# Attention and two gated layers on one core: the integer adds and subtractions of the weight conversions on VectorE, and VectorE's order after the attention as written

## The chip, the core and the metric

The kernel runs on one core of a Trainium2 chip. The core has TensorE (PE, matmuls; PEld is its loading of weights), VectorE (DVE), ScalarE (ACT), GpSimd (POOL) and SyncE (SP), which here issues all DMAs. Each engine takes its own instructions in a fixed order; semaphores hold an instruction until what it needs is there. The metric is the device time of the program in microseconds (us). All times below are us unless marked ns.

## The reference

Four batches of eight heads go through an attention with a window of 128 positions, and the result through two gated layers:

```python
x = attention(q, k, v)             # (4, 8, 576, 64) -> 2304 tokens x 512; window 128, slopes by head
x = ((x @ w_a) * (x @ w_b)) @ w_out            # 512 -> 1536 -> 512
h = ((x @ w1) * (x @ w2)) @ w3                 # 512 -> 1024 -> 1024
out = h @ moe2_w_out                           # 1024 -> 512
```

The weights come as 64-bit floats, read by the kernel as pairs of 32-bit words.

## The kernel before

Every fp32 operand of a matmul is split into a high half, rounded to the matmul's format (fp32r), and a low half, the difference. A product is three matmuls: high x low, low x high, high x high. Layer 1 has six groups of weights (0 to 5) and layer 2 four (6 to 9). A group holds two chunks of 128 columns, each with three parts: of `w_a` (z = 0), of `w_b` (z = 1) and of the output matrix (z = 2), as tiles `whA0`, `wlA0`, `whA1`, `wlA1` for even groups and with B for odd ones. w3 and moe2_w_out are multiplied on the chip to one matrix in two halves (`w34_parts`), and each product goes through DRAM (`w34`); layer 2 adds the halves again (L507).

**A weight's conversion** (`convert`, `split`) makes 128 x 512 fp32 of a `raw` tile of 64-bit words:
- a DMA into `raw`, of which there are two (L82, L91);
- stage s0 on ACT: L107 takes the upper word to `ca` (three buffers), L110 makes a rounding addend `ce` of the lower word (one buffer);
- stage s1 on DVE: L114, L117 and L121 build the fp32 pattern; after L121 and L110 the `raw` is free and its next DMA may start;
- stage s3: L126 adds `ce` to `ca` as integers; then `ce` is free;
- the last stage, `split`: L133 on ACT makes the high half, L72 (in the helper `sub`) the low half. For w3 there are instead four transposes on PE (L437), a high half on ACT (L438), a low half on DVE (L439), and twelve matmuls (L445), whose result ACT copies into a `ce` buffer (L447) for the store to DRAM.

`Stages.turn` advances all conversions that are under way by one stage and starts at most one new; at most three are under way. In the groups a tile of 512 tokens calls it through `side.run` about 3.8 times. Before, L126 and the L72 of conversions ran on POOL, except for group 0's, which ran on DVE (`eng`).

**A group's work on a tile** of 512 tokens: `g1`, four times twelve matmuls (L532) into four PSUM banks; ACT copies a product (L539), DVE multiplies by the other (L541, tile `g`), ACT makes the high half (L544, `gh`) and POOL the low half (L72, `gl`). Then the second product, four banks of six matmuls (L560 in group 0, L571 in groups 1 to 5, L586 after), which DVE adds to `acc` (L575, L593; L591 copies). It runs one tile later, behind the next tile's `g1`. In group 5, ACT and POOL make `x_hi` and `x_lo` of the sum (L577, L72). Group 0 has tiles of 256 tokens; its work fills gaps in the attention, and the rest comes right after it (L740), followed in the text by all of group 1's conversions (L743 to L745) and then by groups 1 to 9 (L751). After the attention there are eight PSUM banks for the matmuls, two in one pool and six in another, taken in turn.

**What sets the order.** A scheduler orders each engine's instructions by dependencies and its own estimates of time. A `manual_schedule` block keeps chosen engines in the order of the text: before, that was PE during the attention alone (L715 to L731). After it all engines, DVE too, were ordered by the scheduler.

Of the kernel before, what the change touches and what calls it, by code (L numbers as in the profile page):

```python
# [16 lines left out]
ALU = mybir.AluOpType  # L17
# [9 lines left out]
def bits(x):  # L27
    return struct.unpack("<f", struct.pack("<I", x))[0]
# [15 lines left out]
def attention_moe_moe(ctx, tc, q, k, v, w_a, w_b, w_o, w_1, w_2, w_3, w_o2, out):  # L44
    nc = tc.nc
# [10 lines left out]
    W = 512  # L56
# [11 lines left out]
    def f32(ap):  # L68
        return ap.bitcast(F32)

    def sub(eng, out, a, b):
        eng.tensor_tensor(out=out, in0=a, in1=b, op=ALU.subtract)  # L72
# [6 lines left out]
    def load_cols(w, c):  # L79

        raw = pools["conv"].tile([P, W, 2], I32, name="raw", bufs=pools["raws"])
        nc.sync.dma_start(  # L82
            out=raw.rearrange("p (k f) t -> p k (f t)", k=KC),
            in_=w[:, c * P:(c + 1) * P].bitcast(I32).rearrange("(k p) f -> p k f", p=P),
        )
        return raw

    def load_rows(w, r, c):

        raw = pools["conv"].tile([P, W, 2], I32, name="raw", bufs=pools["raws"])  # L90
        nc.sync.dma_start(  # L91
            out=raw.rearrange("p f t -> p (f t)"),
            in_=w[r * P:(r + 1) * P, c * W:(c + 1) * W].bitcast(I32),
        )
        return raw

    def convert(raw, hi=None, lo=None, use=(), eng=None):


        hw, lw = raw[:, :, 1], raw[:, :, 0].bitcast(U32)  # L100
        a = pools["conv"].tile([P, W], F32, name="ca", bufs=pools["cas"])
        ai = a.bitcast(I32)
        es = []

        def s0():

            nc.scalar.activation(a, f32(hw), ACTF.Abs)  # L107
            e = pools["conv"].tile([P, W], I32, name="ce", bufs=1)
            es.append(e)
            nc.scalar.activation(e, lw, ACTF.Copy, scale=2.0 ** -29)  # L110

        def s1():

            nc.vector.tensor_scalar(  # L114
                out=a, in0=a, scalar1=bits(0x38000000), scalar2=None, op0=ALU.max
            )
            nc.vector.tensor_scalar(  # L117
                out=ai, in0=ai, scalar1=3, scalar2=0x3FFFFFF8,
                op0=ALU.logical_shift_left, op1=ALU.bitwise_and,
            )  # L120
            nc.vector.scalar_tensor_tensor(  # L121
                out=ai, in0=hw, scalar=-(1 << 30), in1=ai, op0=ALU.bitwise_and, op1=ALU.bitwise_or
            )

        def s3():
            (eng or nc.gpsimd).tensor_tensor(out=ai, in0=ai, in1=es[0], op=ALU.add)  # L126

        if hi is None:
            return [s0, s1, s3] + [lambda f=f: f(a) for f in use]
        return [s0, s1, s3, lambda: split(a, hi, lo, eng)]  # L130

    def split(f, hi, lo, eng=None):
        nc.scalar.activation(hi, f, ACTF.Copy)  # L133
        sub(eng or nc.gpsimd, lo, f, f32(hi))

    class Stages:

# [125 lines left out]
    def prep(run, n):  # L263
        b, (x, i) = blocks_of(run)[0], items(run)[n]
        m = rows(i)
        hold = []

        def trans():
            ps = ps_t.tile([P, W], F32, name="tr")[:, 0:NP * m].rearrange("p (h c) -> p h c", h=NP)
            hold.append(ps)  # L270
            t = raws.pop((b, x, i))
            for hp in range(NP):
                nc.tensor.transpose(ps[:, hp, :], t[0:m, hp * P:(hp + 1) * P], ident[0:m, 0:m])  # L273

        def parted():
            ps = hold[0]
            if x == 0 and m == LAST:
                dst = [(slice(j * D, (j + 1) * D), q_t2, slice(j * D, (j + 1) * D)) for j in range(2)]
            else:
                dst = [(slice(0, P), k_t if x else q_t, slice(i * P, i * P + m))]  # L280
            for o, (hi, lo), c in dst:
                nc.scalar.activation(hi[o, :, c], ps[o], ACTF.Copy)
                sub(nc.vector, lo[o, :, c], ps[o], f32(hi[o, :, c]))

        return trans, parted
# [137 lines left out]
    def w34_parts(pool, halves):  # L423
# [28 lines left out]
        for half in halves:  # L452
            for j in range(NJ):
                parts.append((
                    lambda r=half * NJ + j: load_rows(w_o2, r, 0),
                    lambda raw, j=j: convert(raw, oh[:, j, :], ol[:, j, :]),
                ))
            for f in range(FB):
                parts.append((
                    lambda f=f, half=half: load_rows(w_3, f, half),  # L460
                    lambda raw, f=f, half=half: convert(raw, use=product(half, f)),
                ))
# [10 lines left out]
    def weight_parts(g):  # L473

        blk, chunks = groups[g]
        d = blocks[blk]
        ring = "AB"[g % 2]

        def load(n, z):
            c = chunks[n]  # L480
            if z == 0:
                wt[g, n] = [
                    pools[ring, n].tile([P, 3, KC, P], F32R, name=f"w{s}{ring}{n}", bufs=1) for s in "hl"
                ]
            if z < 2:
                return load_cols(d["ab"[z]], c)
            if blk == 0:
                return load_rows(d["o"], c, 0)
            raw = pools["conv"].tile([P, W, 2], I32, name="raw", bufs=pools["raws"])
            raw = raw.rearrange("p f t -> p (f t)").bitcast(F32)  # L490
            for half in range(2):
                nc.sync.dma_start(
                    out=raw[:, half * W:(half + 1) * W], in_=d["o"][half, c * P:(c + 1) * P, :]
                )
            return raw

        def stages(raw, n, z):
            hi, lo = [t[:, z].rearrange("p k f -> p (k f)") for t in wt[g, n]]

            def count():  # L500
                whole[g] = whole.get(g, 0) + 1

            if z < 2 or blk == 0:
                return convert(raw, hi, lo, eng=None if g else nc.vector) + [count]

            def add():
                nc.gpsimd.tensor_tensor(out=raw[:, 0:W], in0=raw[:, 0:W], in1=raw[:, W:2 * W], op=ALU.add)  # L507

            return [add, lambda: split(raw[:, 0:W], hi, lo), count]

        return [
            (lambda n=n, z=z: load(n, z), lambda raw, n=n, z=z: stages(raw, n, z))
            for n in range(2) for z in range(3)
        ]
# [189 lines left out]
    for x in range(len(items(1))):  # L704
        load_item(1, x)
        f, g = prep(0, x)
# [30 lines left out]
    pools["B", 0] = pools["B", 1] = ctx.enter_context(tc.tile_pool(name="wB", bufs=1))  # L737
    ps_h = ctx.enter_context(tc.tile_pool(name="ps_h", bufs=6, space=PSUM))
    pools["mm"] = [ps_g, ps_h, ps_h, ps_h]
    for f, _, _ in fl.items:  # L740
        side.turn()
        f()
# [35 lines left out]
```

## Time and profile before

| | |
|---|---|
| median of three runs | 977.05 us (974.28 to 977.43) |
| profiled execution | 978.53 us, of which the span is 976.8 |
| PE | busy 944.9 us (97%), 5546 matmuls |
| DVE | 516.5 us (53%) |
| ACT | 417.2 us (43%) |
| POOL | 341.7 us (35%) |
| DMA | 68.30 MB, 24% of 16 engines |
| attention | until about 229 us |
| chain that ended last | PE 84%, DVE 7%, DMA 6%, ACT 2% |

A timeline row has the start, the length, the engine, the line, the operation, output and inputs, and how many in a row; in brackets stands how long the engine was idle before it, and which instruction ended that. "PEclk" is the clock that TensorE was granted, 1.00 for 2.4 GHz and 0.50 for 1.2 GHz. Lengths of matmuls overlap, so that their rate is read from starts.

### The profile page before, as it was taken

The page shows a single profiled execution, that of the slowest core. Times are in us where ns is not written, and L with a number is a line of the kernel's source. Part 1 is how long each engine was busy: PE and PEld are TensorE (multiplying, and loading weights), DVE is VectorE, ACT ScalarE, POOL GpSimd, SP SyncE. Part 2 cuts the span into 40 slices and gives each one's busy share as a digit, 9 for nine tenths or more (in the row PEclk, how much of TensorE's full clock was granted, in tenths as well). Part 3 has the DMA queues.
Part 4 walks back from the last instruction along what each step waited for, and adds up shares of the span by engine and source line. Part 5 has one row for each costly group of instructions (what it writes and reads, how often), then busy time and mean ns, then how long its engine had stood idle before and what let it go on. Part 6 is the DMA issues. An engine that isn't in the chain of part 4 may idle for free.

```text
span 976.8 us, 14512 instructions
## 1 busy us (share of the span) xinstructions
PE 944.9 (97%) x5546; PEld 797.1 (82%) x5546; DVE 516.5 (53%) x1177; ACT 417.2 (43%) x951; POOL 341.7 (35%) x285
## 2 busy tenths in 40 slices
PE   7699999999989999999999999999999999999998
PEld 5487888889777888888888888888888888888886
DVE  6968686865887435756564462542541541421322
ACT  6767787775654323543533441342421321311111
POOL 3000000003776223744542462683831631511111
PEclk8899999999999999999999999999999999999999
DMA  9623231102343122413322330210210210000012
GB/s 212 171 55 74 60 86 40 33 2 94 123 124 114 45 86 76 135 71 98 125 70 84 97 110 1 87 44 1 67 64 1 87 44 0 22 1 1 33 65 97
DMA packets 90373, 68.30 MB, mean 70 GB/s; under 512 B 58304, under 2 KB 79296, under 8 KB 90304
## 3 DMA queue, kind: packets, MB, share of 16 engines
q1 hardware_dynamic: 90304, 67.38, 23.9%
q8 instruction: 43, 0.70, 0.3%
q14 instruction: 26, 0.21, 0.1%
HBM read 58.20 MB, written 8.91 MB: 69 GB/s over the span
## 4 chain that ended last, share of the span: by engine, by line
PE 84%; DVE 7%; DMA 6%; ACT 2%; issue 1%; POOL 0%; SPq 0%; ACTq 0%; DVEq 0%; POOLq 0%
PE mm L532 46%; PE mm L571 11%; PE mm L586 10%; PE mm L445 4%; PE tr L395 3%; PE s L309 2%; DMA raw<-in_moe_w_out 2%; PE tr L374 2%; PE mm L560 2%; PE tr L273 1%; DMA raw<-in_moe_w_b 1%; DVE pe L336 1%; ACT ca L107 1%; DVE pe L356 1%; DVE ca L121 1%; DVE ca L117 1%
## 5 line engine op out<-in xcount | busy, mean ns | idle before, releaser
L72 POOL TENSOR_TENSOR gl<-g,gh 128x512 fp32r<-128x512 f32 (+1 forms) x108 | 123.9, 1147 | 461.2 <-ACT gh L544 461.2
L541 DVE TENSOR_TENSOR g<-a,mm 128x512 f32<-128x512 f32 (+1 forms) x108 | 64.3, 595 | 213.7 <-PE mm L532 197.0
L126 POOL TENSOR_TENSOR ca<-ca,ce 128x512 int32<-128x512 int32 x70 | 91.6, 1309 | 128.0 <-ACT ce L110 68.9
L544 ACT ACTIVATE gh<-g 128x512 fp32r<-128x512 f32 (+1 forms) x108 | 60.3, 558 | 168.6 <-DVE g L541 168.5
L539 ACT ACTIVATE a<-mm 128x512 f32<-128x512 f32 (+1 forms) x108 | 56.0, 519 | 118.9 <-PE mm L532 118.9
L532 PE MATMUL mm<-x_hi,wlA 128*128 128x512 f32 (+1 forms) x464 | 105.9, 349 | 0.0
L532 PE MATMUL mm<-x_hi,wlB 128*128 128x512 f32 (+1 forms) x400 | 99.2, 370 | 3.5 <-DVE g L541 3.2
L532 PE MATMUL mm<-x_lo,whA 128*128 128x512 f32 (+1 forms) x464 | 102.5, 342 | 0.0
L532 PE MATMUL mm<-x_hi,whA 128*128 128x512 f32 (+1 forms) x464 | 101.8, 342 | 0.0
L532 PE MATMUL mm<-x_lo,whB 128*128 128x512 f32 (+1 forms) x400 | 99.2, 370 | 0.0
L532 PE MATMUL mm<-x_hi,whB 128*128 128x512 f32 (+1 forms) x400 | 98.8, 370 | 0.0
L114 DVE TENSOR_SCALAR ca<-ca 128x512 f32<-128x512 f32 x76 | 48.5, 638 | 85.2 <-ACT ca L107 80.0
L532 PEld LDWEIGHTS mm<-x_lo,whA 128*128 128x128 f32 x464 | 76.8, 189 | 10.3
L532 PEld LDWEIGHTS mm<-x_hi,wlA 128*128 128x128 f32 x464 | 76.2, 189 | 10.9 <-issue 0.9
L532 PEld LDWEIGHTS mm<-x_hi,wlB 128*128 128x128 f32 x400 | 71.1, 189 | 17.1 <-DVE g L541 3.8
L532 PEld LDWEIGHTS mm<-x_hi,whA 128*128 128x128 f32 x464 | 76.7, 189 | 10.1
L107 ACT ACTIVATE ca<-raw 128x512 f32<-128x512 f32 x76 | 50.7, 668 | 75.8 <-DMA raw<-in_moe_w 37.9
L532 PEld LDWEIGHTS mm<-x_hi,whB 128*128 128x128 f32 x400 | 71.6, 190 | 12.7
L532 PEld LDWEIGHTS mm<-x_lo,whB 128*128 128x128 f32 x400 | 71.5, 190 | 12.8
L575 DVE TENSOR_TENSOR acc<-acc,mm 128x512 f32<-128x512 f32 (+1 forms) x100 | 62.2, 630 | 36.8 <-PE mm L571 36.5
L121 DVE SCALAR_TENSOR_TENSOR ca<-raw,ca 128x512 int32<-128x512 int32 x76 | 77.6, 1021 | 1.9
L110 ACT ACTIVATE ce<-raw 128x512 int32<-128x512 uint32 x76 | 50.9, 670 | 61.2 <-DMA w<-ce 24.1
(113 smaller groups left out, 1695.2 us busy)
## 6 DMA issues: line engine op xcount, KB each, us to landing
raw<-in_moe_w SPq DMA_DIRECT2D x32, 512.0 KB, 3.6
raw<-in_moe_w_out SPq DMA_DIRECT2D x20, 512.0 KB, 3.6
raw<-in_moe_w_a SPq DMA_DIRECT2D x12, 512.0 KB, 3.7
raw<-in_moe_w_b SPq DMA_DIRECT2D x12, 512.0 KB, 3.8
out<-acc SPq DMA_DIRECT2D x18, 256.0 KB, 2.0
raw<-in_q SPq DMA_DIRECT2D x16, 256.0 KB, 3.1
raw<-in_k SPq DMA_DIRECT2D x16, 256.0 KB, 3.7
v<-in_v SPq DMA_DIRECT2D x16, 256.0 KB, 4.1
```

The costliest lines, as they stand in the source:

```text
L72: eng.tensor_tensor(out=out, in0=a, in1=b, op=ALU.subtract)
L107: nc.scalar.activation(a, f32(hw), ACTF.Abs)
L110: nc.scalar.activation(e, lw, ACTF.Copy, scale=2.0 ** -29)
L121: nc.vector.scalar_tensor_tensor(out=ai, in0=hw, scalar=-(1 << 30), in1=ai, op0=ALU.bitwise_and, op1=ALU.bitwise_or)
L126: (eng or nc.gpsimd).tensor_tensor(out=ai, in0=ai, in1=es[0], op=ALU.add)
L532: nc.tensor.matmul(p, w[:, z, kk, :], x[:, kk, o], start=(y == 0), stop=(y == len(terms) - 1))
L539: nc.scalar.activation(a, ps[0], ACTF.Copy)
L541: nc.vector.tensor_tensor(out=gg, in0=a, in1=ps[1], op=ALU.mult)
L544: nc.scalar.activation(gh, gg, ACTF.Copy)
L571: nc.tensor.matmul(p, w, x, start=(y == 0), stop=(y == len(terms) - 1))
L575: nc.vector.tensor_tensor(out=ya, in0=ya, in1=p, op=ALU.add)
L586: nc.tensor.matmul(p, x, w, start=(y == 0), stop=(y == len(terms) - 1))
```

## The change

L126 and the L72 of `split`, and the addition of the two halves of w34 (L507), are now issued on DVE for all groups. `gl` and `x_lo` stay on POOL. And from the end of the attention on, DVE's instructions are in a `manual_schedule` block to the end of the kernel, so that they stand in the order of the text. PE, ACT, POOL and SP are still ordered by the scheduler, which now knows another DVE.

```diff
-    def convert(raw, hi=None, lo=None, use=(), eng=None):
+    def convert(raw, hi=None, lo=None, use=()):
...
-            (eng or nc.gpsimd).tensor_tensor(out=ai, in0=ai, in1=es[0], op=ALU.add)
+            nc.vector.tensor_tensor(out=ai, in0=ai, in1=es[0], op=ALU.add)
...
-        return [s0, s1, s3, lambda: split(a, hi, lo, eng)]
+        return [s0, s1, s3, lambda: split(a, hi, lo)]
...
-    def split(f, hi, lo, eng=None):
+    def split(f, hi, lo):
         nc.scalar.activation(hi, f, ACTF.Copy)
-        sub(eng or nc.gpsimd, lo, f, f32(hi))
+        sub(nc.vector, lo, f, f32(hi))
...
-                return convert(raw, hi, lo, eng=None if g else nc.vector) + [count]
+                return convert(raw, hi, lo) + [count]
...
-                nc.gpsimd.tensor_tensor(out=raw[:, 0:W], in0=raw[:, 0:W], in1=raw[:, W:2 * W], op=ALU.add)
+                nc.vector.tensor_tensor(out=raw[:, 0:W], in0=raw[:, 0:W], in1=raw[:, W:2 * W], op=ALU.add)
...
     pools["mm"] = [ps_g, ps_h, ps_h, ps_h]
+    ctx.enter_context(tc.manual_schedule(engines={mybir.EngineType.DVE}))
     for f, _, _ in fl.items:
```

The order of the built programs moves as follows; up to the end of the attention it is the same. In the names the numbers are those of buffers, which differ by two between the programs from here on.

First place: DVE right after the attention, where group 0's last products (L541) and group 1's first conversions stand. Before:

```order
L114 TENSOR_SCALAR ca_3646<-ca_3646 128x512
L117 TENSOR_SCALAR ca_3646<-ca_3646 128x512
L121 SCALAR_TENSOR_TENSOR ca_3646<-raw_3642,ca_3646 128x512
L114 TENSOR_SCALAR ca_3655<-ca_3655 128x512
L117 TENSOR_SCALAR ca_3655<-ca_3655 128x512
L121 SCALAR_TENSOR_TENSOR ca_3655<-raw_3644,ca_3655 128x512
L541 TENSOR_TENSOR g_3512<-a_3510,mm_3485 128x256
L114 TENSOR_SCALAR ca_3667<-ca_3667 128x512
L117 TENSOR_SCALAR ca_3667<-ca_3667 128x512
L121 SCALAR_TENSOR_TENSOR ca_3667<-raw_3653,ca_3667 128x512
L541 TENSOR_TENSOR g_3545<-a_3543,mm_3518 128x256
L114 TENSOR_SCALAR ca_3682<-ca_3682 128x512
```

and now:

```order
L541 TENSOR_TENSOR g_3514<-a_3512,mm_3487 128x256
L541 TENSOR_TENSOR g_3547<-a_3545,mm_3520 128x256
L541 TENSOR_TENSOR g_3608<-a_3606,mm_3581 128x256
L114 TENSOR_SCALAR ca_3648<-ca_3648 128x512
L117 TENSOR_SCALAR ca_3648<-ca_3648 128x512
L121 SCALAR_TENSOR_TENSOR ca_3648<-raw_3644,ca_3648 128x512
L126 ISA ca_3648<-ca_3648,ce_3650 128x1024
L114 TENSOR_SCALAR ca_3657<-ca_3657 128x512
L117 TENSOR_SCALAR ca_3657<-ca_3657 128x512
L121 SCALAR_TENSOR_TENSOR ca_3657<-raw_3646,ca_3657 128x512
L72 TENSOR_TENSOR wlB0_3643<-ca_3648,whB0_3642 128x512
L126 ISA ca_3657<-ca_3657,ce_3659 128x1024
```

The three L541 of group 0 now stand ahead of the first L114, and L126 and L72 are among the conversions' instructions, L72 of one conversion behind L114 to L121 of the next.

Second place: PE at the start of group 1 (L532 on `wlB0`, `whB0`), where group 0's last second products (L560) end. Before, with the first matmuls of `whB0` ahead of those L560:

```order
L560 MATMUL mm_3612<-gh_3547,wlA0_236 128x256
L560 MATMUL mm_3626<-gh_3547,wlA0_236 128x256
L532 MATMUL mm_3733<-x_hi_67,wlB0_3641 128x512 x4
L532 MATMUL mm_3733<-x_lo_68,whB0_3640 128x512 x4
L532 MATMUL mm_3733<-x_hi_67,whB0_3640 128x512 x4
L532 MATMUL mm_3746<-x_hi_67,wlB0_3641 128x512 x4
L532 MATMUL mm_3746<-x_lo_68,whB0_3640 128x512 x4
L532 MATMUL mm_3746<-x_hi_67,whB0_3640 128x512 x4
L560 MATMUL mm_3612<-gh_3608,wlA1_313 128x256
L560 MATMUL mm_3612<-gl_3548,whA0_235 128x256
```

and now, with the last L560 first:

```order
L560 MATMUL mm_3628<-gh_3549,whA0_235 128x256
L560 MATMUL mm_3628<-gh_3610,whA1_312 128x256
L532 MATMUL mm_3735<-x_hi_67,wlB0_3643 128x512 x4
L532 MATMUL mm_3735<-x_lo_68,whB0_3642 128x512 x4
L532 MATMUL mm_3735<-x_hi_67,whB0_3642 128x512 x4
L532 MATMUL mm_3748<-x_hi_67,wlB0_3643 128x512 x4
L532 MATMUL mm_3748<-x_lo_68,whB0_3642 128x512 x4
L532 MATMUL mm_3748<-x_hi_67,whB0_3642 128x512 x4
L532 MATMUL mm_3778<-x_hi_67,wlB1_3666 128x512 x4
L532 MATMUL mm_3778<-x_lo_68,whB1_3665 128x512 x4
L532 MATMUL mm_3778<-x_hi_67,whB1_3665 128x512 x4
```

The work is the same; group 0 is now finished before group 1 begins, and the matmuls on `whB1` follow directly on those of `whB0`.

Third place: PE at the fourth of the sixteen w3 products, with the transposes (L437) and the matmuls on `w3l` that come of them (L445). Before:

```order
L571 MATMUL mm_4541<-gh_4296,whB1_3663 128x512
L437 MATMUL mm_4551<-ident_66,ca_4385 128x128 x4
L532 MATMUL mm_4609<-x_hi_67,wlA0_3815 128x512 x4
L532 MATMUL mm_4609<-x_lo_68,whA0_3814 128x512 x4
L532 MATMUL mm_4609<-x_hi_67,whA0_3814 128x512 x4
L445 MATMUL mm_4566<-oh_3723,w3l_4550 128x512 x4
L445 MATMUL mm_4566<-ol_3724,w3h_4549 128x512 x4
```

and now:

```order
L571 MATMUL mm_4543<-gh_4298,whB1_3665 128x512
L437 MATMUL mm_4553<-ident_66,ca_4387 128x128 x4
L445 MATMUL mm_4568<-oh_3725,w3l_4552 128x512 x4
L445 MATMUL mm_4568<-ol_3726,w3h_4551 128x512 x4
L445 MATMUL mm_4568<-oh_3725,w3h_4551 128x512 x4
L532 MATMUL mm_4611<-x_hi_67,wlA0_3817 128x512 x4
L532 MATMUL mm_4611<-x_lo_68,whA0_3816 128x512 x4
```

Before, twelve matmuls of L532 stood between the two; now L445 follows its L437 directly.

## Rows read from the trace of the kernel before

**Rows 1.** Windows: length; busy PE, PEld, DVE, ACT, POOL; PEclk, DMA, GB/s.
```profile
250.00:275.00 25.00, 23.14 (x110) 18.89 (x109) 22.34 (x21) 15.23 (x26) 20.15 (x16) 1.00 0.40 124
...
300.00:325.00 25.00, 23.10 (x107) 18.89 (x106) 15.04 (x25) 9.53 (x16) 12.60 (x10) 0.93 0.25 84
325.00:977.00 652.00, 647.89 (x3112) 545.66 (x3110) 272.83 (x404) 203.71 (x358) 258.83 (x205) 1.00 0.18 60
```

**Rows 2.** Chain that ended last, its end: start, length, what.
```profile
962.01 10.89 PE mm L586 x48
```

**Rows 3.** Timeline of PE from 229 to 321 us, starts of parts and waits.
```profile
229.09 0.51 PE L532 MATMUL mm<-x_lo,whA 128*128 128x256 f32 x3
...
241.70 0.39 PE L560 MATMUL mm<-gl,whA 128*128 128x256 f32 x1 [0.72 <-POOL gl L72]
...
251.23 0.39 PE L560 MATMUL mm<-gl,whA 128*128 128x256 f32 x1 [0.93 <-POOL gl L72]
...
270.38 0.62 PE L571 MATMUL mm<-gh,wlB 128*128 128x512 f32 x2
...
271.88 0.50 PE L571 MATMUL mm<-gl,whB 128*128 128x512 f32 x1 [0.66 <-POOL gl L72]
...
282.61 0.75 PE L532 MATMUL mm<-x_hi,wlB 128*128 128x256 f32 x4 [1.36 <-DVE g L541]
...
309.78 1.29 PE L532 MATMUL mm<-x_hi,wlB 128*128 128x512 f32 x4 [1.83 <-DVE g L541]
...
321.05 0.60 PE L437 MATMUL mm<-ident,ca 128*128 128x128 f32 x4
```

**Rows 4.** Groups by line and shape: count, busy us, mean ns, idle before.
```profile
L126 POOL TENSOR_TENSOR ca<-ca,ce 128x512 int32<-128x512 int32 x70 | 91.6, 1309 | 128.0 <-ACT ce L110 68.9 <-DVE ca L121 34.7 <-issue 10.0
L72 POOL TENSOR_TENSOR wlB<-ca,whB 128x512 fp32r<-128x512 f32 x26 | 36.8, 1424 | 9.2 <-ACT whB L133 9.2
L72 DVE TENSOR_TENSOR wlA<-ca,whA 128x512 fp32r<-128x512 f32 x6 | 4.1, 685 | 0.2 <-ACT whA L133 0.2
L126 DVE CUSTOM_DVE_ANT_0 ca<-ca,ce 128x1024 uint16<-128x1024 uint16 x6 | 4.1, 676 | 0.0
```

**Rows 5.** Timeline of DVE, without POOL at work (first two) and with it.
```profile
233.67 0.43 DVE L117 TENSOR_SCALAR ca<-ca 128x512 int32<-128x512 int32 x1
234.13 0.69 DVE L121 SCALAR_TENSOR_TENSOR ca<-raw,ca 128x512 int32<-128x512 int32 x1
...
256.63 1.41 DVE L117 TENSOR_SCALAR ca<-ca 128x512 int32<-128x512 int32 x1
258.06 1.67 DVE L121 SCALAR_TENSOR_TENSOR ca<-raw,ca 128x512 int32<-128x512 int32 x1
```

**Rows 6.** Timelines: first L114; POOL's `gl`; last L541 of group 0; ACT's `gh`.
```profile
228.37 0.73 POOL L72 TENSOR_TENSOR gl<-g,gh 128x256 fp32r<-128x256 f32 x1 [4.13 <-ACT gh L544]
...
233.20 0.43 DVE L114 TENSOR_SCALAR ca<-ca 128x512 f32<-128x512 f32 x1 [4.13 <-DMA raw<-in_moe_w_b]
...
247.04 0.41 DVE L541 TENSOR_TENSOR g<-a,mm 128x256 f32<-128x256 f32 x1
...
248.13 0.41 ACT L544 ACTIVATE gh<-g 128x256 fp32r<-128x256 f32 x1
```

**Rows 7.** Timeline: a `raw` DMA's issue, and L107, which reads it.
```profile
237.88 0.37 SPq L82 DMA_DIRECT2D raw<-in_moe_w_a  x1
...
241.52 0.68 ACT L107 ACTIVATE ca<-raw 128x512 f32<-128x512 f32 x1 [0.99 <-DMA raw<-in_moe_w_a]
```

**Rows 8.** Windows of PE alone: length, busy PE, PEclk, DMA, GB/s.
```profile
41.05:44.99 3.94, 0.01 (x1) 0.94 0.82 267
44.99:52.00 7.01, 7.01 (x43) 0.55 0.01 5
...
309.78:316.00 6.22, 6.22 (x20) 0.73 0.28 95
```

**Rows 9.** Timeline of DVE: the first L439, behind the L437 of 321.05.
```profile
322.31 0.69 DVE L439 TENSOR_TENSOR w3l<-mm,w3h 128x512 fp32r<-128x512 f32 x1 [0.38 <-ACT w3h L438]
```

## The prediction

> **What bounds the kernel now.** I read the windows by stage first. From 325 us to the end TensorE (PE) is busy 647.89 of 652 us at its full clock; the gaps are in the windows from 250 to 325 us, where it lacks 1.9 of 25 us in the first and in the last, and in the last the granted clock falls to 0.93 [rows 1]. So the end is set by PE's matmuls, and a change that touches VectorE (DVE) and GpSimd (POOL) alone can move it only by what PE waits for them. The attention before 229 us keeps its order, and what follows PE's last matmul is one L593 and a store, both unchanged.
>
> How much is there? 48 matmuls of 512 columns take 10.89 us at the end, 0.2269 each [rows 2]. From 229.09 to 241.70 stand 98 of 256 columns; less the wait of 0.72 they take 11.89 us, 0.121 each [rows 3]. Between 229.09 and the first L571 at 270.38 there are 140 narrow and 96 wide ones: 16.98 + 21.78 = 38.76 us of work in 41.29, so 2.5 are lost. From 270.38 to L437 at 321.05 there are 72 and 150: 42.76 of work in 50.67, so 7.9 are lost (waits of 0.66, 1.36 and 1.83 are the large ones, and after the last PE ran at half clock). **In all 10.4 us can be won at most**, and nothing behind 321 us.
>
> **The change, part by part.**
>
> *Moved work.* 70 integer adds (L126) go from POOL at 1309 ns to DVE, where the six of group 0 took 676; 62 subtractions of conversions (L72) go from about 1424 ns on POOL to 685 on DVE, and 8 additions of L507 with them [rows 4]. That adds 70 x 0.68 + 70 x 0.69 = 96 us to DVE and takes some 190 from POOL.
>
> *What comes back.* L117 takes 0.43 us when POOL is idle and 1.41 while POOL works; L121 0.69 and 1.67 [rows 5]. With POOL left to `gl` and `x_lo` (128 instructions), most of these holds go: L114, L117 and L121 together fall towards 0.43 + 0.43 + 0.69 = 1.55 us. A whole conversion is then about 2.9 us of DVE. A 512-token tile of 48 wide L532 and 24 wide L571 is 16.3 us of PE and has about three conversions (8.7) and six other DVE instructions (6 x 0.69 = 4.1): 12.8 of 16.3. DVE stays covered by PE there.
>
> The Trainium skill (SBUF — State Buffer, "Who interferes with whom") says that a VectorE instruction with two SBUF inputs is blocked for the whole of a GpSimd instruction that reads SBUF, which speaks against this change: L126 and L72 have two such inputs, and `gl` stays on GpSimd. L121 has two and was held [rows 5]; no row shows L126 or L72 beside GpSimd. By the rule the sum below would be 0.7 higher, in the one place where `gl` falls beside them.
>
> *The order at the end of group 0.* Before, the scheduler put the first conversions of group 1 ahead of group 0's last products (L541): the first L114 ran at 233.20 and the last L541 only at 247.04 [rows 6]. Now DVE runs all L541 of group 0 first, and each conversion behind them (first pair of lists in the change). I follow this by hand with the rows' durations.
> - The last L532 of group 0 end after 116 narrow matmuls, 229.09 + 14.0 = 243.1. L541 (0.41), the high half on ScalarE (0.41) and the low half on POOL (0.73) [rows 6], with some 0.3 of handovers, give `gl` at 245.2. PE waits about 1.4 for the two halves, near the 0.72 + 0.93 of before [rows 3], and ends group 0 at 229.09 + 17.0 + 1.4 = 247.5.
> - The first L114 starts at 243.9; L121 ends at 245.6, L126 at 246.4 with a part of a hold. There is one `ce` buffer, so L110 of the second conversion (0.67) waits for this L126, and L133 for L110: 247.7. On DVE the second conversion's L114 to L121 stand ahead of the first one's L72, which ends at 248.7. PE waits 1.2.
> - The second weight needs L72 behind the third conversion's three instructions. Its `raw` is loaded when the first one's is free: from the DMA's issue at 237.88 to L107's start at 241.52 are 3.64 us [rows 7]. So 245.7 + 3.64 + 0.67 + 1.6 + 0.69 = 252.3, with handovers 252.6. PE's twelve matmuls ended at 251.5: 1.1 of wait.
> - The third weight is `whB1`'s first. PE is free at 255.3. On DVE now follow L126 of the third (253.2); L110 and L133 on ScalarE (254.5); L72 of the third (255.2); the fourth conversion with its L126 (257.5); the fifth's three (259.1); and only then L72 of the fourth: 259.7. PE waits 4.4.
>
> The waits add up to 1.4 + 1.2 + 1.1 + 4.4 = **8.1 us**, where 2.5 were lost before. PE stands at the first L571 at about 276.
>
> *The clock.* After a pause of 3.94 us PE ran at a mean of 0.55 for 7.01 us, a loss of 3.15; after the one of 1.83 [rows 3] at a mean of 0.73 for 6.22 us, a loss of 1.7 [rows 8]. The pause of 4.4 is nearest to the first. But if the clock falls already at the shorter pauses, the slow matmuls between them only fill the wait for weights, and nothing is lost. Ends 0 and 3.2; I take **2.0**.
>
> *From 276 to 321 us.* Here the 7.9 us of before can be won. POOL has only `gl` left, so that the waits for `gl` and for held L541 lose their cause. On DVE I get the L575 of the first tile about 5 us behind PE; the eight PSUM banks let PE run two groups of four ahead, about 11 us, so none of it reaches PE. Bounds 0 and 4; I take **0.5**.
>
> *The w3 products behind 321 us, where before nothing is lost.* Two places cost. L437 transposes a `ca`, which now needs L126 on DVE; in the first product this L126 stands behind an L575 of matmuls that PE has just finished, an L72 and itself, 0.1 + 0.6 + 0.6 + 0.7 = 2.0 us after PE's end, while PE has 1.36 us of work in between and loses about **0.9** with the handover. In the fourth product L445 now stands right behind its L437 (third pair of lists). From L437's start at 321.05 to L439's end at 322.31 + 0.69 = 323.00 are 1.95 us [rows 3, 9]; of it PE fills 0.35. It loses 1.6, with DVE's preceding L575 **1.9**. In the other fourteen 2.0 to 7.1 us of PE work lie between the two, enough. Bounds 0 and 5 for both.
>
> The sum: 8.1 + 2.0 + 0.5 + 2.8 = 13.4 lost, against 10.4 before: **+3.0 us**. On the profiled execution (978.53, of which 976.8 is the span) that is 981.5; it lay 1.5 above the median of 977.05, so I say 980.1.
>
> **The rivals.**
>
> *A: the order costs little, and the holds were all.* For it: DVE was busy 22.3 of 25 us from 250 to 275 us [rows 1], much of it in holds, and these are gone. It holds if the third weight comes 3 us earlier (ScalarE and the DMA a little faster than in my chain) and the clock stays up. Then 8.1 + 2.0 becomes about 5, the w3 places stay at about 2, and the sum is 7 against 10.4: 973.6. Against it: the first conversion cannot begin before 243, ten us later than now.
>
> *B: DVE in written order becomes the bound in the tiles with conversions.* Slower. Each instruction now waits at the head of the queue: L72 for L133, L126 for L110, which waits for one `ce`. Covered are 16.3 − 12.8 = 3.5 us a tile; it decides from there on. Two `gl` a tile can each hold one DVE instruction for about 1.0 us [rows 5], which leaves 1.5. If waits at the head take 2.0 a tile, 0.5 us reaches PE in each of some 24 tiles (72 conversions and loads at three a tile): 12 us, less if only the dense ones suffer. I price it at +9: 986. For it: six conversions stand within the first two tiles of group 1, and a w3 conversion waits twice for PE. Against it: 11 us of PSUM slack, and the 272.83 of 652 us that DVE was busy from 325 us on [rows 1], which leaves room on the average.
>
> *C: nothing moves.* That the work is not moved at all is excluded by the list: DVE has the 140 added instructions. That gains and losses cancel is the lower part of my forecast.
>
> **How the numbers follow.** About 0.3%, 2.9 us, is what a measurement of this kernel can tell from no change. My forecast, 980.1 with a range of its own of 976.5 to 983.5, has 0.61; A 0.16; B 0.23. The forecast lies on the 0.3% bound: I give 0.35 of its 0.61 to the same and 0.24 to slower, and 0.02 to faster. A gives 0.13 faster and 0.03 same, B all slower. So faster 0.15, same 0.38, slower 0.47. The range takes in A's middle and most of B: 973.0 to 987.0.
>
> **What would show it.** Right: PE pauses of about 1, 1 and 4 us between 247 and 260 before L532 on `whB`, released by DVE L72; a half clock near 260; the first L571 at 276 to 278; no pause over 1 us from there to 320; L117 near 0.43 us and not at 1.4; a wait of about 1.6 before the fourth L445. Wrong: the first L571 before 273 (then A), or PE waits for DVE L541, L575 or L72 in one tile after the other behind 330 (then B). The weakest term is the pause of 4.4 us with the clock behind it.

## The result

The changed kernel takes 981.18 us (median of 6 runs, 980.57 to 982.01) where the kernel before takes 976.16 beside it (6 runs): a ratio of 1.0052, with a 95% interval of 1.004 to 1.0065, so 3.9 to 6.3 us slower. 980.1 was forecast, in a range of 973 to 987, with slower as the likeliest side. The profiled execution took 981.09 us, of which 978.6 is the span.

The sum had two sides, a loss ahead of 321 us that goes and one that comes. Both are in the trace. First the windows of the changed kernel that answer to [rows 1] (length; busy PE, PEld, DVE, ACT, POOL; granted clock, DMA, GB/s):

```profile
250.00:275.00 25.00, 20.48 (x84) 16.21 (x83) 16.88 (x31) 13.73 (x24) 2.63 (x2) 0.93 0.43 138
300.00:325.00 25.00, 23.66 (x118) 19.83 (x117) 20.67 (x35) 13.07 (x22) 5.30 (x4) 1.00 0.30 98
325.00:977.00 652.00, 648.31 (x3113) 545.95 (x3111) 334.20 (x517) 207.35 (x360) 124.08 (x100) 1.00 0.19 62
```

From 250 to 275 us PE now lacks 4.5 us instead of 1.9, and the granted clock has fallen there (0.93) and not in the last window. Which waits these are, the timeline of PE tells (the attention's last L395, then every row with a wait of PE behind 229 us, the first L571, the last matmuls):

```profile
227.47 0.60 PE L395 MATMUL tr<-pt,v 128*64 128x64 f32 x8
...
244.19 0.38 PE L560 MATMUL mm<-gh,wlA 128*128 128x256 f32 x1 [1.27 <-ACT gh L544]
...
245.19 0.39 PE L560 MATMUL mm<-gl,whA 128*128 128x256 f32 x1 [0.27 <-POOL gl L72]
...
248.69 1.16 PE L532 MATMUL mm<-x_hi,wlB 128*128 128x512 f32 x4 [1.08 <-DVE wlB L72]
...
252.22 1.20 PE L532 MATMUL mm<-x_hi,wlB 128*128 128x512 f32 x4 [0.54 <-DVE wlB L72]
...
259.20 2.08 PE L532 MATMUL mm<-x_hi,wlB 128*128 128x512 f32 x4 [3.97 <-DVE wlB L72]
...
276.98 0.61 PE L571 MATMUL mm<-gh,wlB 128*128 128x512 f32 x2
...
322.53 0.66 PE L437 MATMUL mm<-ident,ca 128*128 128x128 f32 x4 [1.34 <-DVE ca L126]
...
353.25 1.20 PE L445 MATMUL mm<-oh,w3l 128*128 128x512 f32 x4 [1.41 <-DVE w3l L439]
...
974.11 0.61 PE L586 MATMUL mm<-whB,gh 128*128 128x512 f32 x2
```

Three waits for weights of group 1 stand where there was one of 0.27, none from 277 to 321 us, where there were 0.66, 1.36 and 1.83 [rows 3] and one of 0.35, and two new ones at the w3 products. Behind 353 us PE waits for nothing.

Since PE's matmuls are the same in all kernels here (in each stretch the same number of each width), their starts cut every trace at three points: the attention's last row of L395, the first L571, and the last row of L586. Between these lie two stretches:

| | last L395 | to the first L571 | on to the last L586 |
|---|---|---|---|
| before, first profile | 227.94 | 42.44 | 701.89 |
| before, second profile | 226.55 | 42.43 | 701.56 |
| after | 227.47 | 49.51 | 697.13 |

So the change costs 7.1 us in the first stretch and gives back 4.4 to 4.8 in the second, a net 2.3 to 2.7. The rest of the measured 5.0 lies in neither. Where the attention ended differed from one profile to the next, from 226.48 to 229.13 over all kernels here, though its order there is the same; the last section shows where a part of this comes from.

### The profile page after: what moved, and what is told of

It is laid out like the page before. It is cut to its first block, busy times and chain, and to the rows that moved or that the text cites. A ratio compares the mean times of both kernels' runs of the same rounds, so it can differ in the third digit from the quotient of the medians.

```text
span 978.6 us, 14447 instructions
## 1 busy us (share of the span) xinstructions
PE 943.3 (96%) x5546; PEld 797.4 (81%) x5546; DVE 571.5 (58%) x1317; ACT 419.0 (43%) x951; POOL 159.2 (16%) x145
## 4 chain that ended last, share of the span: by engine, by line
PE 90%; DVE 6%; ACT 2%; DMA 1%; issue 1%; SPq 0%; DVEq 0%; ACTq 0%
PE mm L532 51%; PE mm L571 12%; PE mm L586 10%; PE mm L445 4%; PE tr L395 3%; PE s L309 2%; PE mm L560 2%; PE tr L374 2%; PE tr L273 1%; DVE pe L336 1%; DVE pe L356 1%; ACT pe L342 1%; PE mm L437 1%; DVE ca L121 1%; DMA raw<-in_k 0%
## 5 line engine op out<-in xcount | busy, mean ns | idle before, releaser
L72 POOL TENSOR_TENSOR gl<-g,gh 128x512 fp32r<-128x512 f32 (+1 forms) x108 | 125.9, 1166 | 802.3 <-ACT gh L544 802.3
L541 DVE TENSOR_TENSOR g<-a,mm 128x512 f32<-128x512 f32 (+1 forms) x108 | 64.4, 597 | 228.1 <-PE mm L532 195.1
L539 ACT ACTIVATE a<-mm 128x512 f32<-128x512 f32 (+1 forms) x108 | 55.9, 521 | 135.2 <-PE mm L532 134.8
L532 PE MATMUL mm<-x_hi,wlA 128*128 128x512 f32 (+1 forms) x464 | 105.9, 348 | 0.0
L532 PE MATMUL mm<-x_hi,wlB 128*128 128x512 f32 (+1 forms) x400 | 99.7, 371 | 5.6 <-DVE wlB L72 5.6
L532 PE MATMUL mm<-x_lo,whA 128*128 128x512 f32 (+1 forms) x464 | 102.7, 342 | 0.0
L532 PE MATMUL mm<-x_hi,whA 128*128 128x512 f32 (+1 forms) x464 | 102.0, 342 | 0.0
L532 PE MATMUL mm<-x_lo,whB 128*128 128x512 f32 (+1 forms) x400 | 98.9, 369 | 0.0
L532 PE MATMUL mm<-x_hi,whB 128*128 128x512 f32 (+1 forms) x400 | 98.7, 368 | 0.0
L107 ACT ACTIVATE ca<-raw 128x512 f32<-128x512 f32 x76 | 51.1, 672 | 95.1 <-DMA raw<-in_moe_w 37.1
L532 PEld LDWEIGHTS mm<-x_hi,wlB 128*128 128x128 f32 x400 | 71.5, 190 | 19.1 <-DVE wlB L72 5.4
L532 PEld LDWEIGHTS mm<-x_hi,wlA 128*128 128x128 f32 x464 | 76.3, 189 | 11.1 <-issue 0.9
L532 PEld LDWEIGHTS mm<-x_lo,whA 128*128 128x128 f32 x464 | 76.7, 189 | 10.1
L532 PEld LDWEIGHTS mm<-x_hi,whA 128*128 128x128 f32 x464 | 76.6, 189 | 10.0
L532 PEld LDWEIGHTS mm<-x_lo,whB 128*128 128x128 f32 x400 | 71.6, 190 | 12.8
L532 PEld LDWEIGHTS mm<-x_hi,whB 128*128 128x128 f32 x400 | 71.0, 189 | 12.4
L110 ACT ACTIVATE ce<-raw 128x512 int32<-128x512 uint32 x76 | 50.7, 668 | 70.6 <-DVE ca L126 46.5
L342 ACT ACTIVATE pe<-pe,st 128x256 f32<-128x256 f32 (+1 forms) x144 | 68.2, 477 | 15.2 <-DVE st L336 14.6
L575 DVE TENSOR_TENSOR acc<-acc,mm 128x512 f32<-128x512 f32 (+1 forms) x100 | 60.1, 629 | 23.2 <-PE mm L571 23.0
L126 DVE CUSTOM_DVE_ANT_0 ca<-ca,ce 128x1024 uint16<-128x1024 uint16 x76 | 63.1, 831 | 3.3 <-ACT ce L110 3.1
L121 DVE SCALAR_TENSOR_TENSOR ca<-raw,ca 128x512 int32<-128x512 int32 x76 | 59.5, 783 | 2.4
```

What stands on the lines that cost most here:

```text
L121: nc.vector.scalar_tensor_tensor(out=ai, in0=hw, scalar=-(1 << 30), in1=ai, op0=ALU.bitwise_and, op1=ALU.bitwise_or)
L126: nc.vector.tensor_tensor(out=ai, in0=ai, in1=es[0], op=ALU.add)
L342: nc.scalar.activation(pe[:, j, :n], pe[:, j, :n], ACTF.Exp, bias=st[:, 0, j:j + 1], scale=-1.0, accum_out=st[:, 1, j:j + 1],)
L532: nc.tensor.matmul(p, w[:, z, kk, :], x[:, kk, o], start=(y == 0), stop=(y == len(terms) - 1))
L539: nc.scalar.activation(a, ps[0], ACTF.Copy)
L541: nc.vector.tensor_tensor(out=gg, in0=a, in1=ps[1], op=ALU.mult)
```

## The experiments

They form three questions: which half of the change costs, where it costs, and what the moved work gives back by which mechanism. Each time is a median beside the kernel before on the same chip (977.28 in the first four, 977.0 in the next four, 976.73 in the last).

### The halves apart: ops_only and order_only

```diff
 # ops_only, against the changed kernel
-    ctx.enter_context(tc.manual_schedule(engines={mybir.EngineType.DVE}))
```

> The changed kernel without its written order for VectorE: the additions and subtractions are on VectorE, and the scheduler places them, so that group 1's conversions stand among group 0's last products again. My theory (the late conversions between 243 and 277 us cost about 7 us, VectorE's added work costs nothing and the vanished holds behind 277 us give back about 5): no wait of TensorE on whB or wlB over 0.5 us before the first L571, which comes at 269 to 271 us, no half clock near 260, L117 near 0.5 us; 966 to 972 us against 976.2 of the kernel before. Rival 1 (VectorE's added 96 us of work, beside gl on GpSimd, is the cost, wherever the scheduler puts it): 979 to 982, with TensorE waiting for VectorE behind 277 us. Rival 2 (the moved work does nothing, only the order counts): 975 to 977.5.

Measured: **967.93 us, ratio 0.9903 (0.9886 to 0.9921)**, and a second time, on another chip, 968.52 against 976.73. This is faster than both kernels, as the theory had it (the first L571 comes at 268.3, a little ahead of its 269), and both rivals fall. The moved work alone is worth 8 to 9 us, and PE has next to no wait left (the rows of PE, and the window of [rows 1]):

```profile
227.70 0.60 PE L395 MATMUL tr<-pt,v 128*64 128x64 f32 x8
...
241.39 0.39 PE L560 MATMUL mm<-gl,whA 128*128 128x256 f32 x1 [0.28 <-POOL gl L72]
...
268.33 0.62 PE L571 MATMUL mm<-gh,wlB 128*128 128x512 f32 x2
...
962.24 0.61 PE L586 MATMUL mm<-whB,gh 128*128 128x512 f32 x2
```
```profile
250.00:275.00 25.00, 25.00 (x125) 21.23 (x125) 23.30 (x38) 16.50 (x30) 4.22 (x3) 1.00 0.45 144
```

Its stretches are 40.63 and 693.91 us, and 693.91 came out again in the second profile. From the first L571 to the end this is PE at work without a gap. The written order, then, costs about 981.2 − 968 = 13 us beside the moved work.

```diff
 # order_only, against the kernel before
     pools["mm"] = [ps_g, ps_h, ps_h, ps_h]
+    ctx.enter_context(tc.manual_schedule(engines={mybir.EngineType.DVE}))
```

> The kernel before with the written order for VectorE alone; the additions and subtractions stay on GpSimd. My theory: the late conversions cost more than in the changed kernel, since an addition takes 1.31 us and a subtraction 1.42 where VectorE takes 0.7 to 0.8, and gl stands in the same queue: the first L571 at 279 to 285 us, and the holds of L117 and L121 stay (1.4 and 1.7 us beside GpSimd): 984 to 992 us. Rival 1 (the moved work is the cost, the order is free): 975 to 977.5. Rival 2 (GpSimd's own queue, written in the scheduler's order, lets the conversions through as early as before): 975 to 979.

Measured: 981.27 us, ratio 1.0042 (1.0028 to 1.0056), faster than my 984 to 992. Half of the theory held, half fell. The two long waits for weights (each followed by eight matmuls at about half their rate) and the first run of L571:

```profile
250.92 1.88 PE L532 MATMUL mm<-x_hi,wlB 128*128 128x512 f32 x4 [3.28 <-POOL wlB L72]
...
261.15 1.89 PE L532 MATMUL mm<-x_hi,wlB 128*128 128x512 f32 x4 [2.88 <-POOL wlB L72]
...
279.42 0.62 PE L571 MATMUL mm<-gh,wlB 128*128 128x512 f32 x2
```

L571 is late, as foreseen (one of them had run at 268.31; the run starts at 279.42). But the second stretch is 693.9 us, as good as in ops_only, although the additions and subtractions are on POOL and DVE's instructions are still held there, as its timeline shows:

```profile
280.69 1.40 DVE L117 TENSOR_SCALAR ca<-ca 128x512 int32<-128x512 int32 x1
282.12 1.66 DVE L121 SCALAR_TENSOR_TENSOR ca<-raw,ca 128x512 int32<-128x512 int32 x1
```

So the holds alone do not make PE wait. In the kernel before PE waited where the scheduler had put a conversion ahead of an L541, and for the longest pause, 1.83 us at 309.78, a hold was the smaller part. DVE sat idle for 1.83 us before the next conversion's L114, which needs L107 and so a loaded `raw`, with the L541 behind it (both operands of which had been there since 304.89, when L539 ended):

```profile
308.70 0.43 DVE L114 TENSOR_SCALAR ca<-ca 128x512 f32<-128x512 f32 x1 [1.83 <-ACT ca L107]
309.05 0.68 DVE L541 TENSOR_TENSOR g<-a,mm 128x512 f32<-128x512 f32 x1
```

The two halves also do not add up to the whole. On the kernel before, the written order costs 4.0 us (981.27 against 977.28) and not 13; and under the written order moving the work changes nothing in the medians (981.27 and 981.18), where under the scheduler's it gives 8 to 9. In the traces it shortens the first stretch there, which is 51.9 us in order_only, by 2.2 (one L571 of the second stretch, 0.23, runs in the first of order_only) and lengthens the second by 3.0, at the w3 products.

### The place: early, late and tail_order

```diff
 # early, against the changed kernel
+    side.parts += weight_parts(1)
     for f, _, _ in fl.items:
         side.turn()
         f()
-    side.parts += weight_parts(1)
```

> The changed kernel with one line of the text moved: group 1's weights are handed to the side work ahead of the loop over group 0's remaining items, so that in the written order its conversions stand among group 0's last products. My theory (the place costs, not the written order as such): TensorE's waits of 1.16, 1.20 and 2.08 us for wlB and the half clock behind them go, the first L571 comes at 270 to 272 us, the two waits behind 321 us stay (1.3 and 1.4): 973 to 976 us against 981.2 of the changed kernel. Rival (the waits only change their name: group 0's products L541 and with them gh and gl now wait behind conversions at the head of VectorE's queue): TensorE waits for gh, gl or g between 229 and 250 us, and the time is 978 to 982.

Measured: 980.54 us, ratio 1.0032 (1.002 to 1.0043). My theory fell and the rival held: the waits only changed their name. DVE's timeline ahead of one of group 0's last L541, with PE's row that waits for its `gh`:

```profile
240.91 0.68 DVE L126 CUSTOM_DVE_ANT_0 ca<-ca,ce 128x1024 uint16<-128x1024 uint16 x1
243.04 0.69 DVE L72 TENSOR_TENSOR wlB<-ca,whB 128x512 fp32r<-128x512 f32 x1 [1.44 <-ACT whB L133]
...
245.17 0.41 DVE L541 TENSOR_TENSOR g<-a,mm 128x256 f32<-128x256 f32 x1
```
```profile
246.09 0.58 PE L560 MATMUL mm<-gh,wlA 128*128 128x256 f32 x1 [6.14 <-ACT gh L544]
```

Its operands were there by 239.9 at the latest: the last L539 ahead of it ended at 237.18, and PE's matmuls stop at 239.9 until 246.09. L541 stood another five microseconds behind conversions: behind their own work, and behind L72, which at the head of DVE's queue waited 1.44 us for ACT. Its first stretch is 50.18 us, no better than the 49.51 of the changed kernel.

```diff
 # late, against the changed kernel
     pools["mm"] = [ps_g, ps_h, ps_h, ps_h]
-    ctx.enter_context(tc.manual_schedule(engines={mybir.EngineType.DVE}))
 ...
     gate_a.close()
+    ctx.enter_context(tc.manual_schedule(engines={mybir.EngineType.DVE}))
```

> The changed kernel with VectorE's written order beginning only behind group 1's conversions: the scheduler orders the end of group 0 as in the kernel before, and the text orders all from there on, the w3 products among it. My theory: the first L571 at 269 to 272 us, then as in the changed kernel: the two waits of TensorE behind 321 us (for L126 at the first w3 product, for L439 at the fourth) with about 2.8 us in all; 970 to 975 us. Rival 1 (the written order costs at every tile with conversions): 978 to 982. Rival 2 (the two w3 places cost nothing, since TensorE would lose the time elsewhere): the same as the kernel with the moved work alone, within 1 us.

Measured: 971.95 us, ratio 0.9951 (0.9935 to 0.9966): 9.2 us below the changed kernel, and 4.0 above ops_only. The stretches are 40.46 and 697.11: the first as without the written order, the second as in the changed kernel (697.13). PE's only waits behind 245 us are the same two at the w3 products, 1.34 and 1.41 again. This is what the theory gave, and both rivals fall. So 9 us of the written order's cost lie at the end of group 0, and 3 to 4 behind it. In none of these kernels is PE's order held fixed: the scheduler changes it with DVE's, as the lists of the change show, so the cost is that of both together.

```diff
 # tail_order, against ops_only
-    for f, _, _ in gate_items(range(1, NG), cuts(TN), 1):
+    for x, (f, _, _) in enumerate(gate_items(range(1, NG), cuts(TN), 1)):
+        if x == 120:
+            ctx.enter_context(tc.manual_schedule(engines={mybir.EngineType.DVE}))
         f()
```

> The moved work with the scheduler's order up to and past the last w3 product, and VectorE's written order only from there (behind 545 us) to the end. If the written order costs nothing outside the end of group 0 and the w3 products: as the kernel without it, within 1 us, 967 to 969. If it costs a little in every tile with weight conversions: the remaining 24 of them would cost it 1 to 2 us, 969 to 970.5.

Measured: 968.64 us beside 968.52 of ops_only, second stretch 693.91 in both. Behind the w3 products the written order costs nothing.

### The w3 products: late_w3pool

```diff
 # late_w3pool, against late
         def s3():
-            nc.vector.tensor_tensor(out=ai, in0=ai, in1=es[0], op=ALU.add)
+            (nc.vector if hi is not None else nc.gpsimd).tensor_tensor(out=ai, in0=ai, in1=es[0], op=ALU.add)
```

> The kernel whose written order begins behind group 1's conversions, with one more edit: the additions of the w3 conversions are back on GpSimd; the others stay on VectorE. TensorE's own order changes with it at one place: the fourth w3 product's L445 no longer stands right behind its L437. My theory (the 4.0 us between 971.95 and 967.93 are the two TensorE waits of 1.34 and 1.41 us at the w3 products with what follows from them, and the written order costs nothing else): both waits gone, 967.5 to 969.5 us. Rival (the written order costs at many places, too little at each for a wait to show): 970.5 to 972.5, though both waits are gone.

Measured: 970.1 us, ratio 0.9927 (0.9911 to 0.9943), between the two forecasts. It was measured a second time, beside ops_only:

> The written order behind group 1's conversions with the w3 additions on GpSimd, once more on the chip of the two above, since 970.1 lay between what the two theories gave. If the two w3 places are all: within 1 us of the kernel without written order on this chip. If the written order costs elsewhere too, or the additions on GpSimd take back a part: 1.5 to 2.5 us above it, as before.

> The kernel with the moved work and the scheduler's order once more, beside the next one and the one with the w3 additions on GpSimd, on the same chip. Expected by both theories: 967 to 969 us.

Measured: 969.71 against 968.52. Both waits are gone in both profiles, and the second stretch is 694.25 and 694.32, where late has 697.11 and ops_only 693.91. The traces give the two places 2.8 to 2.9 of the 3.2 us. The times agree less well: 1.2 us stay, against 0.4 in the trace. The other 0.8 are not explained; the intervals of the two ratios overlap (0.9916 to 0.9941 and 0.9906 to 0.9933).

### What the moved work gives: adds_only, subs_only, gl_dve

```diff
 # adds_only, against the kernel before
-            (eng or nc.gpsimd).tensor_tensor(out=ai, in0=ai, in1=es[0], op=ALU.add)
+            nc.vector.tensor_tensor(out=ai, in0=ai, in1=es[0], op=ALU.add)
 # subs_only, against the kernel before (and L507 on nc.vector)
-        sub(eng or nc.gpsimd, lo, f, f32(hi))
+        sub(nc.vector, lo, f, f32(hi))
```

> The kernel before with the integer additions (L126) alone on VectorE; subtractions stay on GpSimd, the scheduler sets the order. It takes 70 x 1.31 = 92 us from GpSimd and adds about 50 to VectorE. Theory 1 (the loss of the kernel before is VectorE held by GpSimd and falls with GpSimd's work): about half of the gain of 9.4 us, 971 to 974. Theory 2 (a conversion's latency through GpSimd's queue is the loss, and one trip less is enough): 967.5 to 970. Theory 3 (only both together help): 975 to 978.

> The kernel before with the conversions' subtractions (L72 on wl and ol) and L507 alone on VectorE; the additions stay on GpSimd, the scheduler sets the order. It takes 62 x 1.42 = 88 us and L507 from GpSimd and adds about 50 to VectorE. Theory 1 (holds in proportion to GpSimd's work): about half of the gain, 971 to 974. Theory 2 (one trip through GpSimd's queue less is enough): 967.5 to 970. Theory 3 (only both together): 975 to 978.

Measured: 974.46 (0.9969, 0.9957 to 0.9981) and 974.37 (0.9971, 0.9961 to 0.998). Each gives 2.6 us, both together 8 to 9. That is at the edge between the first theory and the third: the halves do not add up, each leaves most of the loss standing. The first stretches are 43.34 and 39.74, the second 697.39 and 700.58. In subs_only DVE is still held by POOL (the L121 beside a `gl`, the L114 beside an L126), with an L541 behind the held instructions, and PE behind that (DVE's rows, then PE's):

```profile
273.54 1.67 DVE L121 SCALAR_TENSOR_TENSOR ca<-raw,ca 128x512 int32<-128x512 int32 x1
...
275.73 1.52 DVE L114 TENSOR_SCALAR ca<-ca 128x512 f32<-128x512 f32 x1
...
278.35 0.68 DVE L541 TENSOR_TENSOR g<-a,mm 128x512 f32<-128x512 f32 x1
```
```profile
279.09 0.74 PE L532 MATMUL mm<-x_hi,wlB 128*128 128x256 f32 x4 [1.98 <-DVE g L541]
```

The first stretch of subs_only, 39.74 us, is the shortest of all: PE waits for nothing in it. 39.74 and 693.91 serve below as the two stretches without loss. Whether a hold or the longer way of a conversion through POOL's queue makes the second stretch longer, these two runs do not tell apart.

```diff
 # gl_dve, against ops_only
-        sub(nc.gpsimd, gl, gg, f32(gh))
+        sub(nc.vector, gl, gg, f32(gh))
```

> The changed kernel without its written order, with gl on VectorE too, so that GpSimd has only x_lo's 36 late subtractions left behind 229 us. If GpSimd's reads are what lengthens VectorE's instructions, L126 falls from 742 ns to about 680, L121 from 767 to 690, L117 from 488 to 430 and L72 on wlB from 773 to 690; if the lengthening comes from elsewhere they stay. My theory for the time: TensorE has no wait left to lose behind 229 us, so 967 to 969.5. Rival (gl now stands behind conversions in VectorE's queue, and TensorE waits for it): 970 to 976 with waits for gl from VectorE.

Measured: 969.32 us, ratio 0.9919 (0.9906 to 0.9932). Groups of DVE by line (count, busy us, mean ns, idle before), first of ops_only, then of gl_dve:

```profile
L126 DVE CUSTOM_DVE_ANT_0 ca<-ca,ce 128x1024 uint16<-128x1024 uint16 x76 | 56.4, 742 | 12.4 <-ACT ce L110 9.9
L121 DVE SCALAR_TENSOR_TENSOR ca<-raw,ca 128x512 int32<-128x512 int32 x76 | 58.2, 767 | 1.5
```
```profile
L126 DVE CUSTOM_DVE_ANT_0 ca<-ca,ce 128x1024 uint16<-128x1024 uint16 x76 | 52.3, 688 | 13.0 <-ACT ce L110 10.9
L121 DVE SCALAR_TENSOR_TENSOR ca<-raw,ca 128x512 int32<-128x512 int32 x76 | 52.3, 689 | 1.3
```

With `gl` off POOL the lengthening goes, to 688, 689 and, for L117, from 488 to 425 ns. (L72 on `wlB` kept a mean of 755: its median is 690, and the few long ones stand around 680 us, beside POOL's `x_lo`.) So POOL's instructions are what holds DVE's. But PE gets nothing from it: the second stretch is 693.91 as before, and the first grows to 42.13, with a wait of 0.6 for `gl`, which now stands in DVE's queue, and one of 0.9 for `gh`, which ACT began 1.35 us after its L541, behind an L110, an L133 and an L563. The rival was right on the wait for `gl`, and the time came out in the theory's range.

### A second look at the kernel before

> The kernel before, a second profile, since its first one (978.53) lay above the median of its runs. If the pause of 1.83 us at 309.78 with the lower clock behind it (about 3.5 us together) is not in every execution: a span of 972 to 974 without it, or 976 to 977 with it. If every execution has it, the spans differ elsewhere, in the attention ahead of 229 us.

Measured: 976.81 us, span 975.0. PE's rows:

```profile
226.55 0.60 PE L395 MATMUL tr<-pt,v 128*64 128x64 f32 x8
...
308.11 2.07 PE L532 MATMUL mm<-x_hi,wlB 128*128 128x512 f32 x4 [2.29 <-DVE g L541]
...
970.54 0.61 PE L586 MATMUL mm<-whB,gh 128*128 128x512 f32 x2
```

The pause for the late L541, 1.83 in [rows 3], is there again with 2.29, again with an L114 ahead of L541 that DVE was idle for (2.28 us), and the matmuls behind it run at half rate; so it belongs to this kernel and not to one execution. The spans differ mainly in the attention, which ended 1.39 us earlier.

## Why the prediction was right

The signs that the prediction named for being right came: three pauses before L532 on group 1's weights, released by DVE's L72, the half clock from 259 us on, the first L571 at 276.98, no pause from there to 320, and a wait before the fourth L445. Against the stretches without loss (39.74 and 693.91) the terms can be set beside what they came to:

| term | forecast | measured |
|---|---|---|
| before: lost up to the first L571 | 2.5 | 2.7 |
| before: lost from there on | 7.9 | 7.7 and 8.0 |
| after: waits at the end of group 0, with the clock | 8.1 + 2.0 | 9.8 |
| after: from there to 321 us | 0.5 | no wait |
| after: the two w3 places | 2.8 | 3.2 |
| net | +3.0 | +2.3 to +2.7 in the traces; +5.0 in the medians |

*The waits.* Forecast were 1.4, 1.2, 1.1 and 4.4, in sum 8.1. The rows have 1.27 + 0.27, 1.08, 0.54 and 3.97, in sum 7.1. (The parts given for the first `gl` add up to 244.95, not 245.2; the row has 245.14, and no other term changes by it.) The large one is the chain that the prediction drew, with L72 of the fourth conversion ending at 259.1 where 259.7 stood in the sum (DVE's rows, between them ACT's):

```profile
256.33 0.69 DVE L126 CUSTOM_DVE_ANT_0 ca<-ca,ce 128x1024 uint16<-128x1024 uint16 x1
257.11 0.67 ACT L110 ACTIVATE ce<-raw 128x512 int32<-128x512 uint32 x1 [1.20 <-DVE ca L126]
257.70 0.61 ACT L133 ACTIVATE whB<-ca 128x512 fp32r<-128x512 f32 x1
257.86 0.69 DVE L121 SCALAR_TENSOR_TENSOR ca<-raw,ca 128x512 int32<-128x512 int32 x1
258.46 0.68 DVE L72 TENSOR_TENSOR wlB<-ca,whB 128x512 fp32r<-128x512 f32 x1
```

*The clock.* Eight matmuls from 259.20 to 262.47 ran at a mean granted clock of 0.56 (window of PE alone):

```profile
259.20:262.47 3.27, 3.27 (x8) 0.56 0.47 163
```

They took 3.27 us instead of 8 x 0.2269 = 1.82. With 0.1 lost behind each of the two shorter pauses, where the granted clock stayed at 1.00, that is 1.7, against 2.0. Waits and this make 8.8 of the 9.8. Most of the last microsecond is the rows' way of counting: a pause begins at the end of the matmul before it, and a wide one is 0.39 long in the profile where the next starts after 0.23, so that each of the five pauses costs some 0.16 more than its row says. The sum had no such term; that 10.1 was forecast and 9.8 came is in part luck, waits 1.0 too long against this 0.8 that was missing.

*From 277 to 321 us* the whole loss of the kernel before went, as forecast, and L117 fell from 796 to 507 ns. The reason given for it was too narrow. The prediction had PE's waits lose "their cause" with the holds. But order_only keeps the holds and loses nothing there either, and at the longest of these pauses the largest part of L541's delay was an L114 that waited for a load. What the rows of subs_only and of the kernel before show is a conversion that is late, held or waiting, and an L541 queued behind it. The work off POOL (ops_only) or another order (order_only), either is enough. What decides it in order_only, the place of L541 in the queue or group 1's conversions having been finished earlier against PE, was not told apart.

*The w3 products.* 0.9 and 1.9 were forecast, 1.34 and 1.41 came; that the sums agree is luck. The first was sized too small because its L72 was held by a `gl`: POOL's row, and DVE's two ahead of L437 (322.53):

```profile
320.03 1.29 POOL L72 TENSOR_TENSOR gl<-g,gh 128x512 fp32r<-128x512 f32 x1 [2.91 <-ACT gh L544]
```
```profile
320.47 1.40 DVE L72 TENSOR_TENSOR ol<-ca,oh 128x512 fp32r<-128x512 f32 x1
321.79 0.68 DVE L126 CUSTOM_DVE_ANT_0 ca<-ca,ce 128x1024 uint16<-128x1024 uint16 x1
```

The prediction had 0.6 for this L72. The hold adds 0.7 to it. The Trainium skill (SBUF — State Buffer, "Who interferes with whom") says that a VectorE instruction with two SBUF inputs contends with a GpSimd instruction that reads SBUF, and that the order of issue decides which of the two is blocked; the prediction told only the one side of it. The traces agree, for L72 here, which began behind the `gl` (1.40 us against 0.69), and for L126 on the mean (742 ns in ops_only, 688 with `gl` off GpSimd). The prediction gave that rule 0.7 us in sum and took the sum without it, which was the wrong side. In the fourth product the 1.95 us from L437's start to L439's end came out as forecast (351.24 to 353.19); the 0.3 added for an L575 did not, since that one ended at 352.13, before ACT's L438 was done.

*The rivals.* B, DVE in written order as the bound tile after tile, is refuted: no wait of PE behind 353 us, and tail_order costs nothing, though DVE was busy 334 of the 652 us from 325 on, against 273 before [rows 1]. A failed at the point that it named: the third weight came 0.6 us earlier than in the sum, not 3. But its idea that the moved work is worth much was right by itself, and larger than A had it: without the written order the time is 968, not 973.6.

*What was not covered.* The medians differ by 5.0 us, 2.4 to 2.7 more than the two stretches account for. Between the second profile of before (976.81) and that of after (981.09) the difference of 4.28 is 7.08 and −4.43 for the two stretches, 0.92 for the attention, 0.7 for what lies around the span. That 0.7 belongs to the one execution: over all runs 1.8 us lie outside the span in the median, in both kernels. The changed kernel's profile is also one of its shortest runs, with a span of 978.6 where the median of its six is 979.2; that of before is 974.9 in 38 runs. So 4.3 us of span stand against 2.3 to 2.7 in the two stretches. The rest has no part in the change that a row shows; whether it shifts with the change is open. The forecast of +3.0 lies between them, and its sum covers only the two stretches.

## What to carry to other kernels

Moving work off a slower engine and fixing an order by hand are two changes; time each without the other (here 968 us with the moved work alone, 981.3 with the order alone, 981.2 with both, 977 with neither), since a loss of 0.5% hid a gain of 0.9%, and what one is worth depends on the other. An order as written puts everything that waits, for a load, a buffer or another engine, at the head of the queue for whatever stands behind it, so look first at the seams where one phase's last products meet the next phase's first loads: nearly all of the cost stood at one seam and two products, and at most 0.4 us in the regular tiles. And moving the waiting work to the other side of what waits behind it does not help unless the two are interleaved by when they are ready, as early showed beside late.

## What the runs showed of the hardware

Two things were not expected. The start differs between two executions of one kernel: in the window from 45 to 52 us the granted clock was 0.55 in the first profile of the kernel before [rows 8] and, in the second, 0.76 (PE alone):

```profile
45.00:52.00 7.00, 7.00 (x55) 0.76 0.12 47
```

PE had 12 more instructions in that window (55 against 43), and the attention ended 1.39 us earlier. Counted by PE's instructions, the two profiles are 0.12 us apart at the 201st (38.8 us in the first profile) and 1.42 at the 301st (56.2 us), and they keep that distance to the attention's end. And the holds of DVE, about 1 us for one instruction (1.67 us instead of 0.69 [rows 5]), can be there or not without a change of PE's time: with `gl` on DVE the 76 L121 fell to 689 ns, the 0.69 us that [rows 5] shows without POOL, and with conversions on POOL in order_only they still took 912 ns (1021 in the kernel before); PE's second stretch was 693.9 us in both.
